# Attention and two feed-forward layers: one output copy on ScalarE, its halves moved by GpSimd, a longer argmax chain, four score products in a slot

## The chip, the cores and the metric

One core of a Trainium2 chip. The metric is the device time of one execution in microseconds. The engines are named TensorE (PE, with PEld for its weight loads), VectorE (DVE), ScalarE (ACT), GpSimd (POOL) and SyncE (SP, which here only issues DMAs).

## The reference

Three stages follow each other: a clustered attention, and two feed-forward layers that differ in their function. Batch 2, 8 heads, 768 positions, head size 64, 16 centroids per head; 1536 tokens, model width 512, hidden width 2048.

```python
q_assign = np.argmax(np.einsum('bhsd,hcd->bhsc', q_n, c_n), axis=-1)   # normalised q, centroids
k_assign = np.argmax(np.einsum('bhsd,hcd->bhsc', k_n, c_n), axis=-1)
mask = q_assign[:, :, :, None] == k_assign[:, :, None, :]
scores = scale * np.matmul(q, k.transpose(0, 1, 3, 2))
scores = np.where(mask, scores, -1000000000.0)
scores = scores - np.max(scores, axis=-1, keepdims=True)
attn = np.exp(scores)
attn = attn / (np.sum(attn, axis=-1, keepdims=True) + 1e-09)
out = np.matmul(attn, v)
...
h = x @ w_in;  g = h * np.cos(h);  x = g @ w_out                       # first layer
g = np.where(pos, h, np.where(neg, 0.0, (h + beta) ** 2 / (4.0 * beta))) # second layer
```

## The kernel before

Every product is made in parts: a value is split into a high part of type fp32r and the rest, so that products of the parts add up to more than fp32r alone gives.

**Attention** goes over 8 pairs of heads (batch x 4). A pair has four units, one for each head h and half hf of its 768 queries, in the order (h0,hf0), (h0,hf1), (h1,hf0), (h1,hf1): 32 units. A unit has six slots, one for each block of 128 keys: 192 slots, and the loop at the end of the stage runs over them. A block n of 128 queries (three in a unit, 96 in all) gets four score products of 384 columns in two steps (`scores`, L471 and L474, tile s, two buffers of two PSUM banks), a maximum over 768 scores on VectorE (`row_max`, L480, tile nm), and an exp on ScalarE (`row_exp`, L489, tile p, six buffers). It is worked on 8 slots (LEAD) ahead of the slot that uses it. In a slot, `p_transpose` turns three 128x128 pieces of p on TensorE (L517, tile pt; the pool ps_t has three banks, which pt shares with the tiles of the preparation and with r), ScalarE copies them as high part phi (L520), and VectorE makes the low part plo (L525, `p_lo`, for two slots at a time in every even slot). `p_v` multiplies phi and plo with the values (L535, L536) into tile o, of which there is one bank; PV_AT lists at which slot after a unit's first each of its six key blocks is multiplied.

When the last of the six is in, `o_parts` empties o. The bank holds 128 rows: the 64 of this head and 64 of the other part of the values. ScalarE copies each half on its own (L549, 64x384) into the rows of this head of two tiles xt0 and xt1, so that for both heads of a pair xt0 and xt1 come to hold what has to be added. Two slots later `finish` transposes the reciprocals rb (L559, tile r), adds the two tiles on GpSimd (L561), multiplies by r on VectorE (L562), and GpSimd splits the result into xh and xl (L565, L569), the input of the first layer. `inverse` makes the reciprocals of the row sums (L499, L500) and GpSimd spreads each of three columns over 64 (L504).

Beside that, `prep_pair` prepares the next pair in small steps, one for each `yield` and slot: transposes of q and k (L329, L337), their parts on GpSimd (L301, L302), DMAs on SP's queue that stack them (L315), the load of the next q and k (L208), products with the centroids (L367, L368, tile pd), their sums (L356, tile dots), and the argmax chain: maximum (L413), compare (L415), a product with falling numbers on GpSimd (L416), maximum (L421), equality (L423). Then come the parts of v (L436, L437), the transposes of the one-hot rows (L446, tile po), their copy (L448, tile oht) and eight DMAs of it into the stacks (L292). A preparation starts PREP slots before the pair ahead of it does (PREP1 for the first).

`later(n, f)` puts a function off until the n-th next call of `next_slot`, of which there is one in each slot, after the value products; `later(1, ...)` from `p_v` so runs in the same slot. The program's text gives the order in which steps are preferred; the order in which each engine gets them is planned when the program is built, and each engine then keeps to it. Weights of the layers are converted by `pump` in steps (L144 to L160), the first twelve in the last 36 slots of attention.

**The layers** (L670 to L672, 512 columns each) follow; TensorE starts the first of them while the last outputs of attention are still being finished.

Of the kernel before, what the change touches and what calls it, by code (L numbers as in the profile page):

```python
# [8 lines left out]
F32 = mybir.dt.float32  # L9
# [4 lines left out]
AF = mybir.ActivationFunctionType  # L14
ALU = mybir.AluOpType
# [3 lines left out]
P = 128  # L19
# [13 lines left out]
def attention_moe_moe(  # L33
# [18 lines left out]
    nc = tc.nc  # L52
    B, H, S, D = q.shape
# [4 lines left out]
    HJ = NJ // 2  # L58
    HS = S // 2
# [9 lines left out]
    cpool = ctx.enter_context(tc.tile_pool(name="cpool", bufs=1))  # L69
# [2 lines left out]
    desc = cpool.tile([P, C], F32, name="desc")  # L72
    for c in range(C):
        nc.gpsimd.memset(desc[:, c:c + 1], float(C - c))
    ones = cpool.tile([P, D], F32, name="ones")
    nc.gpsimd.memset(ones, 1.0)
    ohscale = cpool.tile([P, 1], F32, name="ohscale")
    ohbias = cpool.tile([P, 1], F32, name="ohbias")
    for r in range(4):
# [25 lines left out]
    def later(n, f, *args):  # L105
        due.setdefault(now[0] + n, []).append((f, args))
# [85 lines left out]
    with ExitStack() as actx:  # L192
        ap = actx.enter_context(tc.tile_pool(name="apool", bufs=1))
# [82 lines left out]
        def prep_pair(i):  # L276
# [3 lines left out]
            t = nat[i][0]  # L280
            if i in (1, 3, 5):
                t2 = w0pool.tile([P, 2, 2, S], F32R, tag="w_0", name=f"t2_{i}")
# [78 lines left out]
            for s in range(2):  # L361
                pd = ps_t.tile([P, NJ, 2, 2, C], F32, tag="t", name=f"pd{i}_{s}")
                for j in range(NJ):
                    cols = slice(j * P, (j + 1) * P)
                    o = pd[:, j].rearrange("p t h c -> p (t h c)")
# [11 lines left out]
            if i == 0:  # L377
                run_idle(NIDLE[2], ins(mm))
                for s in range(2):
                    dv = dotv[s]  # L380
                    m = mx[:, s * G // 2:(s + 1) * G // 2].rearrange("p (j h) -> p j h", h=2)
                    e = eq[:, s * G // 2:(s + 1) * G // 2].rearrange("p (j h) c -> p j h c", h=2)
                    mb = m.unsqueeze(3).to_broadcast([P, NJ, 2, C])
                    db = desc.unsqueeze(1).unsqueeze(1).to_broadcast([P, NJ, 2, C])
                    nc.vector.tensor_reduce(m, dv, AX.X, ALU.max)
                    nc.vector.tensor_tensor(e, dv, mb, ALU.is_ge)
                    nc.vector.tensor_tensor(e, e, db, ALU.mult)
                    nc.vector.tensor_reduce(m, e, AX.X, ALU.max)
                    nc.vector.tensor_tensor(dv, e, mb, ALU.is_equal)

                    po = ps_t.tile([P, HJ, P], F32, tag="t", name=f"po0_{s}")
                    for jp in range(HJ):
                        mm = nc.tensor.transpose(
                            po[:4 * C, jp],
                            dv[:, 2 * jp:2 * jp + 2].rearrange("p r h c -> p (r h c)"), ident)
                    run_idle(NIDLE[3 + s], ins(mm))
                    for h in range(2):
                        for par in range(2):
                            r0 = par * 2 * C
                            dst = st[h][s][D:D + 2 * C, 1].rearrange(  # L400
                                "c (jp par n) -> c jp par n", par=2, n=P)[:, :, par]
                            src = po[r0:r0 + 2 * C]
                            if s == 0:
                                nc.scalar.activation(dst, src, AF.Copy)
                            else:
                                nc.vector.tensor_scalar(
                                    dst, src, own[r0:r0 + 2 * C, 0, h:h + 1],
                                    own[r0:r0 + 2 * C, 1, h:h + 1], ALU.mult, ALU.add)
            else:
                dv = dots.rearrange("p j s h c -> p (j s h) c")  # L410
                mb = mx.unsqueeze(2).to_broadcast([P, G, C])
                yield
                nc.vector.tensor_reduce(mx, dv, AX.X, ALU.max)  # L413
                yield
                nc.vector.tensor_tensor(eq, dv, mb, ALU.is_ge)  # L415
                nc.gpsimd.tensor_tensor(  # L416
                    eq, eq, desc.unsqueeze(1).to_broadcast([P, G, C]), ALU.mult)
                yield
                yield
                yield  # L420
                nc.vector.tensor_reduce(mx, eq, AX.X, ALU.max)  # L421
                yield
                nc.vector.tensor_tensor(dv, eq, mb, ALU.is_equal)  # L423
                yield
            if i == 0:
                with tc.issue_after(ins(last[0])):
# [34 lines left out]
        def scores(n, step):  # L461

            i, h, hf = units[n // HJ]
            j = hf * HJ + n % HJ
            qt, kt = prepped[i][1][h]
            if step == 0:
                ptile[n] = ps_s.tile([P, 2, 512], F32, tag="s", name=f"s{n}")
            s = ptile[n]
            cols = slice(j * P, (j + 1) * P)
            kc = slice(step * HS, (step + 1) * HS)  # L470
            nc.tensor.matmul(s[:, step, :HS], qt[:, 0, cols], kt[:, 0, kc],  # L471
                             start=True, stop=False)
            rows = D + C if i else D + 2 * C
            nc.tensor.matmul(s[:, step, :HS], qt[:rows, 1, cols], kt[:rows, 1, kc],  # L474
                             start=False, stop=True)

        def row_max(n):
            nm = ap.tile([P, 1], F32, tag="nm", bufs=8, name=f"nm{n}")
            s = ptile[n]
            nc.vector.tensor_reduce(nm, s[:, :, :HS], AX.XY, ALU.max, negate=True)  # L480
            ptile[n] = (s, nm)

        def row_exp(n):
            s, nm = ptile[n]
            u, jj = divmod(n, HJ)
            if jj == 0:
                dens[u] = ap.tile([P, HJ, 2], F32, tag="den", bufs=4, name=f"den{u}")
            p = ap.tile([P, 2, HS], F32, tag="p", bufs=P_BUFS, name=f"p{n}")
            nc.scalar.activation(p, s[:, :, :HS], AF.Exp, bias=nm,  # L489
                                 accum_out=dens[u][:, jj, 0:1])  # L490
            ptile[n] = p
            if jj == HJ - 1:
                later(2, inverse, u)

        def inverse(u):

            i, h, hf = units[u]
            den = dens.pop(u)
            nc.gpsimd.tensor_scalar(den[:, :, 0], den[:, :, 0], 1e-9, 1.0, ALU.add, ALU.mult)  # L499
            nc.vector.reciprocal(den[:, :, 1], den[:, :, 0])  # L500
            if h == 0:
                rb[(i, hf)] = ap.tile([P, HJ, 2, D], F32, tag="rb", bufs=2, name=f"rb{i}_{hf}")
            for jj in range(HJ):
                nc.gpsimd.tensor_scalar(rb[(i, hf)][:, jj, h], ones, den[:, jj, 1:2], 1.0,  # L504
                                        ALU.mult, ALU.mult)

        dens = {}
        rb = {}
        pts = {}
        xt = {}  # L510
# [29 lines left out]
        def o_parts(u):  # L540
            i, h, hf = units[u]
            o = opsum.pop(u)
            main = slice(h * D, (h + 1) * D)
            other = slice((1 - h) * D, (2 - h) * D)
            if h == 0:
                xt[(i, hf)] = [ap.tile([P, HS], F32, tag=f"xt{n}", bufs=2,
                                       name=f"xt{n}_{i}_{hf}") for n in range(2)]
            for t, rows in zip(xt[(i, hf)], (main, other)):
                nc.scalar.activation(t[main], o[rows], AF.Copy)  # L549
            if h == 1:  # L550
                later(2, finish, i, hf)

        def finish(i, hf):
            b, hp = pairs[i]
# [16 lines left out]

        LEAD, PREP, PREP1 = 8, 12, -3
        PV_AT = (4, 4, 5, 6, 7, 8)
        NSLOT = len(units) * NJ
        PAIR = 4 * NJ
        ct = centroid_load()
# [15 lines left out]
        for slot in range(-max(LEAD, PREP), NSLOT + PV_AT[-1] - NJ + 1):  # L594
            g = slot + LEAD
            if slot in prep_at:
                preps.append(prep_pair(prep_at[slot]))
            if 0 <= slot < NSLOT:
                p_transpose(slot // NJ, slot % NJ)
            if 0 <= g < NSLOT:  # L600
                scores(g // 2, g % 2)
            for u, kt in pv_slots.get(slot, ()):
                p_v(u, kt)
            if slot % 2 == 0:
                for s in (slot - 1, slot):
                    if 0 <= s < NSLOT:
                        p_lo(s // NJ, s % NJ)
                if 2 <= g < NSLOT + 2:
                    row_exp(g // 2 - 1)
            next_slot()  # L610
            if slot == 60:
                issue_chunk(0)
            preps = [p for p in preps if next(p, 0) != 0]
            if NSLOT - 6 * CHUNK <= slot < NSLOT and slot % 3 == 0:
                pump(1)
            if slot % 2 == 1 and 0 <= g < NSLOT:
                row_max(g // 2)
        flush()


# [100 lines left out]
    for l in range(2):  # L721
        for qi in range(NQ):
            for blk in range(NB):
                g = hidden(l, qi, blk)
# [35 lines left out]
```

## Time and profile before

| | before |
|---|---|
| time, median of 3 runs | 823.03 us (818.95 to 823.06) |
| profiled execution: its time, its span | 821.92 us, 819.9 us |
| TensorE busy | 801.3 us (98%), 4042 matmuls |
| VectorE, ScalarE, GpSimd busy | 633.6 (77%), 416.5 (51%), 271.5 us (33%) |
| granted TensorE clock | full in all of the 40 slices |

The page's slices show the stages: attention from about 22 to 284 us, with VectorE and ScalarE at eight to nine tenths and GpSimd at three to seven; then the layers, with ScalarE at two to four tenths and TensorE full. A busy share of TensorE is read with care: records of matmuls overlap and their ends are modelled, so that the spacing of their starts tells more than their length.

### The profile page before, as it was taken

The numbers are of one execution on the slowest core, as the hardware profiler recorded it, in microseconds if no ns is written. First come the engines' busy times: TensorE is split into PE (matmuls) and PEld (weight loads), VectorE is DVE, ScalarE is ACT, GpSimd is POOL, SyncE is SP. The second block draws the span as 40 slices with busy tenths as digits, with TensorE's granted clock in tenths as the row PEclk, the third lists the DMA queues.
The fourth block names the chain that finished last, engine by engine and source line by source line (L and its number), as shares of the span: only waits on it lengthen the run. The fifth ranks groups of instructions, "written<-read, shape, count | busy, mean of one in ns | idle before, by whom it ended". The sixth has DMA issues, their size and how long they took to land.

```text
span 819.9 us, 11334 instructions
## 1 busy us (share of the span) xinstructions
PE 801.3 (98%) x4042; PEld 669.9 (82%) x4042; DVE 633.6 (77%) x957; ACT 416.5 (51%) x794; POOL 271.5 (33%) x442
## 2 busy tenths in 40 slices
PE   8899999999999999999999999999999999999998
PEld 5788988988888887888888888888888888888886
DVE  4889899899898687787878878887876987755552
ACT  3688888897979764444343424323434333222220
POOL 3356665577553341222211221442231122111110
PEclk9999999999999999999999999999999999999999
DMA  7666556446540002222131312122112122000012
GB/s 155 153 131 142 134 129 167 101 105 137 138 88 34 1 13 92 102 68 87 51 104 52 103 56 98 52 81 74 52 54 100 52 78 76 1 1 0 14 49 92
DMA packets 48183, 65.97 MB, mean 80 GB/s; under 512 B 27904, under 2 KB 32640, under 8 KB 48128
## 3 DMA queue, kind: packets, MB, share of 16 engines
q1 hardware_dynamic: 47984, 65.22, 29.2%
q8 instruction: 32, 0.52, 0.3%
q14 instruction: 23, 0.19, 0.1%
q10 hardware_dynamic: 144, 0.03, 0.0%
HBM read 43.02 MB, written 3.15 MB: 56 GB/s over the span
## 4 chain that ended last, share of the span: by engine, by line
PE 62%; DVE 1%; ACT 1%; POOL 1%; issue 0%; POOLq 0%
PE y L672 11%; PE y L671 11%; PE y L670 11%; PE h L672 10%; PE h L671 10%; PE h L670 10%; DVE gl L632 0%; DVE r L640 0%; POOL gh L628 0%; DVE g L645 0%; ACT L641 0%; ACT r L641 0%; DVE w L160 0%; ACT n L639 0%; ACT wx L144 0%
## 5 line engine op out<-in xcount | busy, mean ns | idle before, releaser
L628 POOL TENSOR_SCALAR gh<-g 128x512 fp32r<-128x512 f32 x96 | 71.2, 742 | 292.9 <-DVE g L659 165.7
L671 PE MATMUL h<-xl,w 128*128 128x512 f32 x384 | 151.4, 394 | 0.0
L670 PE MATMUL h<-xh,w 128*128 128x512 f32 x384 | 151.4, 394 | 0.0
L672 PE MATMUL h<-xh,w 128*128 128x512 f32 x384 | 151.3, 394 | 0.0
L525 DVE TENSOR_TENSOR plo<-pt,phi 128x384 fp32r<-128x384 f32 x192 | 99.9, 548 | 17.2 <-ACT phi L520 16.2
L520 ACT ACTIVATE phi<-pt 128x384 fp32r<-128x384 f32 x192 | 91.8, 494 | 21.6 <-PE pt L517 19.8
L655 ACT ACTIVATE p<-h,mone 128x512 f32<-128x512 f32 x48 | 33.1, 689 | 134.5 <-DVE m L654 134.1
L517 PE MATMUL pt<-ident,p 128*128 128x128 f32 x576 | 96.5, 277 | 3.4 <-ACT oht L448 1.6
L480 DVE TENSOR_REDUCE nm<-s 128x1 f32<-128x768 f32 x96 | 90.7, 947 | 6.2 <-PE s L474 5.8
L489 ACT ACTIVATE p<-s,nm 128x768 f32<-128x768 f32 x96 | 86.9, 905 | 10.4 <-DVE nm L480 10.1
L632 DVE TENSOR_TENSOR gl<-g,gh 128x512 fp32r<-128x512 f32 x96 | 71.1, 742 | 20.3 <-POOL gh L628 15.3
L672 PEld LDWEIGHTS h<-xh,w 128*128 128x128 f32 x384 | 71.8, 187 | 17.7
L671 PEld LDWEIGHTS h<-xl,w 128*128 128x128 f32 x384 | 71.8, 187 | 17.6
L670 PEld LDWEIGHTS h<-xh,w 128*128 128x128 f32 x384 | 71.8, 187 | 17.5
L144 ACT ACTIVATE wx<-wraw 128x1024 f32<-128x1024 f32 x32 | 36.4, 1138 | 95.0 <-DMA wraw<-in_moe_w_in_dram 35.4
L471 PE MATMUL s<-st,st 128*128 128x384 f32 x192 | 78.1, 408 | 4.1 <-ACT p L489 3.6
L517 PEld LDWEIGHTS pt<-ident,p 128*128 128x128 f32 x576 | 69.9, 140 | 12.4 <-ACT oht L448 3.3
L672 PE MATMUL y<-gh,w 128*128 128x512 f32 x192 | 74.8, 390 | 1.2 <-DVE w L160 1.2
L671 PE MATMUL y<-gl,w 128*128 128x512 f32 x192 | 74.8, 390 | 0.0
L671 PE MATMUL y<-w,gh 128*128 128x512 f32 x192 | 74.8, 390 | 0.0
L670 PE MATMUL y<-gh,w 128*128 128x512 f32 x192 | 74.8, 389 | 0.0
L670 PE MATMUL y<-w,gh 128*128 128x512 f32 x192 | 74.7, 389 | 0.0
(120 smaller groups left out, 1629.2 us busy)
## 6 DMA issues: line engine op xcount, KB each, us to landing
wraw<-in_moe_w_in_dram SPq DMA_DIRECT2D x16, 1024.0 KB, 5.2
wraw<-in_moe_w_out_dram SPq DMA_DIRECT2D x16, 1024.0 KB, 4.9
st<-t SPq DMA_DIRECT2D x24, 192.0 KB, 4.1
st<-th SPq DMA_DIRECT2D x9, 384.0 KB, 3.8
st<-tl SPq DMA_DIRECT2D x18, 192.0 KB, 4.0
st<-th SPq DMA_DIRECT2D x18, 192.0 KB, 3.2
nat<-in_q_dram SPq DMA_DIRECT2D x8, 384.0 KB, 5.2
nat<-in_k_dram SPq DMA_DIRECT2D x8, 384.0 KB, 5.2
```

The costliest lines, as they stand in the source:

```text
L144: nc.scalar.activation(x, high.bitcast(F32), AF.Abs)
L471: nc.tensor.matmul(s[:, step, :HS], qt[:, 0, cols], kt[:, 0, kc], start=True, stop=False)
L480: nc.vector.tensor_reduce(nm, s[:, :, :HS], AX.XY, ALU.max, negate=True)
L489: nc.scalar.activation(p, s[:, :, :HS], AF.Exp, bias=nm, accum_out=dens[u][:, jj, 0:1])
L517: nc.tensor.transpose(ps[:, jj * P:(jj + 1) * P], p[:, kt * P:(kt + 1) * P], ident)
L520: nc.scalar.activation(hi, ps, AF.Copy)
L525: nc.vector.tensor_tensor(lo, ps, hi.bitcast(F32), ALU.subtract)
L628: nc.gpsimd.tensor_scalar(hi, g, 1.0, 0.0, ALU.mult, ALU.add)
L632: nc.vector.tensor_tensor(lo, g, hi.bitcast(F32), ALU.subtract)
L670: nc.tensor.matmul(o, lh, rh, start=first, stop=False)
L671: nc.tensor.matmul(o, lh, rl, start=False, stop=False)
L672: nc.tensor.matmul(o, ll, rh, start=False, stop=last)
```

## The change

Six edits, all in attention:

- `o_parts` copies the whole bank, 128x384, by one ScalarE instruction into a tile of the head: xt0 for the first, xt1 for the second.
- A new function `o_rows`, a slot after the second head's copy, has GpSimd copy three halves of 64 rows so that two tiles come to hold what is to be added: the first head's other half and the second head's other half change rows into a new tile xt2 and xt1. `finish` comes a slot after that, so at the same slot as before.
- `inverse` fills the 3 x 64 columns of rb by one GpSimd instruction that reads the three reciprocals in a broadcast, instead of three that multiply a tile of ones; the tile of ones goes.
- The argmax chain has three more waiting slots, and PREP is 15 for 12, PREP1 -6 for -3.
- Both steps of a block's scores, four products, come in the even slots; the maximum follows at the end of the same slot and the exp at the end of the odd one.
- PV_AT is (5, 5, 6, 7, 8, 8) for (4, 4, 5, 6, 7, 8).

```diff
-    ones = cpool.tile([P, D], F32, name="ones")
-    nc.gpsimd.memset(ones, 1.0)
...
                 yield
                 yield
                 yield
+                yield
                 nc.vector.tensor_reduce(mx, eq, AX.X, ALU.max)
                 yield
                 nc.vector.tensor_tensor(dv, eq, mb, ALU.is_equal)
+                yield
+                yield
                 yield
...
-            for jj in range(HJ):
-                nc.gpsimd.tensor_scalar(rb[(i, hf)][:, jj, h], ones, den[:, jj, 1:2], 1.0,
-                                        ALU.mult, ALU.mult)
+            nc.gpsimd.tensor_scalar(
+                rb[(i, hf)][:, :, h], den[:, :, 1].unsqueeze(2).to_broadcast([P, HJ, D]),
+                1.0, 0.0, ALU.mult, ALU.add)
...
-            if h == 0:
-                xt[(i, hf)] = [ap.tile([P, HS], F32, tag=f"xt{n}", bufs=2,
-                                       name=f"xt{n}_{i}_{hf}") for n in range(2)]
-            for t, rows in zip(xt[(i, hf)], (main, other)):
-                nc.scalar.activation(t[main], o[rows], AF.Copy)
+
+            t = ap.tile([P, HS], F32, tag=f"xt{h}", bufs=2, name=f"xt{h}_{i}_{hf}")
+            xt.setdefault((i, hf), []).append(t)
+            nc.scalar.activation(t, o, AF.Copy)
             if h == 1:
-                later(2, finish, i, hf)
+                later(1, o_rows, i, hf, main, other)
+
+        def o_rows(i, hf, main, other):
+            t0, t = xt[(i, hf)]
+            t2 = ap.tile([P, HS], F32, tag="xt2", bufs=1, name=f"xt2_{i}_{hf}")
+            xt[(i, hf)] = (t, t2)
+            for dst, rows, src in ((t2, other, t0[main]), (t2, main, t[other]), (t, other, t0[other])):
+                nc.gpsimd.tensor_scalar(dst[rows], src, 1.0, 0.0, ALU.mult, ALU.add)
+            later(1, finish, i, hf)
...
-        LEAD, PREP, PREP1 = 8, 12, -3
-        PV_AT = (4, 4, 5, 6, 7, 8)
+        LEAD, PREP, PREP1 = 8, 15, -6
+        PV_AT = (5, 5, 6, 7, 8, 8)
...
-            if 0 <= g < NSLOT:
-                scores(g // 2, g % 2)
+            if 0 <= g < NSLOT and g % 2 == 0:
+                scores(g // 2, 0)
+                scores(g // 2, 1)
             for u, kt in pv_slots.get(slot, ()):
                 p_v(u, kt)
             if slot % 2 == 0:
                 for s in (slot - 1, slot):
                     if 0 <= s < NSLOT:
                         p_lo(s // NJ, s % NJ)
-                if 2 <= g < NSLOT + 2:
-                    row_exp(g // 2 - 1)
             next_slot()
...
-            if slot % 2 == 1 and 0 <= g < NSLOT:
-                row_max(g // 2)
+            if 0 <= g < NSLOT:
+                (row_exp if g % 2 else row_max)(g // 2)
```

## Rows read from the trace of the kernel before

**Rows 1.** Busy time of each engine, 40 to 280 us: us (x instructions).

```profile
40.00:280.00 240.00, 231.44 (x1536) 208.72 (x1535) 213.66 (x368) 203.72 (x453) 136.73 (x243) 1.00 0.49 113
```

**Rows 2.** Timeline of TensorE, 150 to 153 us: start, us, instruction.

```profile
150.37 0.49 PE L517 MATMUL pt<-ident,p 128*128 128x128 f32 x3
...
151.40 0.49 PE L517 MATMUL pt<-ident,p 128*128 128x128 f32 x3
...
152.58 0.28 PE L367 MATMUL pd<-cn,t 128*128 128x64 f32 x1
152.69 0.28 PE L368 MATMUL pd<-cn,t 128*128 128x64 f32 x1
```

**Rows 3.** TensorE's groups, 40 to 280 us: line, shapes, count, busy, mean ns, idle before.

```profile
L517 PE MATMUL pt<-ident,p 128*128 128x128 f32 x542 | 90.3, 277 | 2.8 <-ACT oht L448 1.6 <-DVE plo L525 1.3
L471 PE MATMUL s<-st,st 128*128 128x384 f32 x176 | 71.9, 409 | 2.6 <-ACT p L489 2.0
L535 PE MATMUL o<-phi,vv 128*128 128x384 f32 x181 | 66.2, 366 | 2.4 <-ACT xt L549 2.3
```

**Rows 4.** Waits, 40 to 280 us: who for whom, us, times, longest.

```profile
PEld s L471 <- ACT p L489: 7.5, 19, 0.6
PEld o L535 <- ACT xt L549: 6.8, 16, 0.7
...
PEld pt L517 <- ACT oht L448: 3.3, 7, 0.5
...
PE o L535 <- ACT xt L549: 2.3, 7, 0.4
...
PE s L471 <- ACT p L489: 2.0, 9, 0.4
PE pt L517 <- ACT oht L448: 1.6, 6, 0.3
```

**Rows 5.** Timeline, 131 to 136 us: a unit's end, its bank, its output.

```profile
131.28 0.34 PE L536 MATMUL o<-plo,vv 128*128 128x384 f32 x1
...
131.65 0.98 ACT L549 ACTIVATE xt<-o 64x384 f32<-64x384 f32 x2 [0.16 <-PE o L536]
...
132.69 0.44 PE L535 MATMUL o<-phi,vv 128*128 128x384 f32 x1 [0.39 <-ACT xt L549]
...
135.46 0.56 DVE L562 TENSOR_TENSOR xt<-xt,r 128x384 f32<-128x384 f32 x1
```

**Rows 6.** GpSimd's groups, 40 to 280 us.

```profile
L504 POOL TENSOR_SCALAR rb<-ones,den 128x64 f32<-128x64 f32 x90 | 28.7, 338 | 5.1 <-DVE den L500 4.6 <-DMA st<-oht 0.6
...
L436 POOL TENSOR_SCALAR vv<-natv 128x384 fp32r<-128x384 f32 x12 | 6.0, 512 | 0.8 <-PE o L536 0.8
```

**Rows 7.** The chain of work that ended last, 284 to 312 us: its add.

```profile
285.85 1.02 POOL xt L561
```

**Rows 8.** Waits, 284 to 312 us.

```profile
PE y L672 <- DVE w L160: 1.2, 1, 1.2
```

**Rows 9.** Two lines of VectorE, whole run: duration in ns, min/median/max.

```profile
L415 DVE TENSOR_TENSOR eq<-dots,mx x7: 546/727/1097, 42.5 to 229.9; 128x384 f32<-128x384 f32 x7
...
L413 DVE TENSOR_REDUCE mx<-dots x7: 514/553/554, 41.2 to 227.7; 128x24 f32<-128x384 f32 x7
```

**Rows 10.** Timeline, 120 to 132 us: VectorE and ScalarE at maxima and exps.

```profile
120.53 1.01 DVE L525 TENSOR_TENSOR plo<-pt,phi 128x384 fp32r<-128x384 f32 x2
120.64 0.90 ACT L489 ACTIVATE p<-s,nm 128x768 f32<-128x768 f32 x1 [1.08 <-DVE nm L480]
...
121.45 0.95 DVE L480 TENSOR_REDUCE nm<-s 128x1 f32<-128x768 f32 x1
...
121.77 0.49 ACT L520 ACTIVATE phi<-pt 128x384 fp32r<-128x384 f32 x1
...
122.44 0.90 ACT L489 ACTIVATE p<-s,nm 128x768 f32<-128x768 f32 x1 [0.17 <-DVE nm L480]
...
123.33 0.48 ACT L520 ACTIVATE phi<-pt 128x384 fp32r<-128x384 f32 x1
```

## Prediction

> **What bounds the kernel now.** I began with the page's busy shares (TensorE 98%) and its chain of work, which is TensorE through both feed-forward layers from about 310 us on; no edit reaches them, so what matters is the attention stage. There I took the busy time of each engine in the stretch 40 to 280 us [rows 1]: TensorE 231.4 of 240 us, VectorE 213.7, ScalarE 203.7, GpSimd 136.7. A busy TensorE is not a full one, so next comes what it would need without a wait. In an undisturbed slot the transposes of one slot start 1.03 us after those of the slot before, with three transposes and four products of 384 columns between; the 64-column products follow each other by 0.11 us [rows 2]. The stretch holds 542 transposes of the probabilities, 2 x 176 score products and 2 x 181 value products [rows 3], that is 542 / 3 = 180.7 slots x 1.03 = 186.1 us; the other 279 small instructions (1536 less these and one of the next stage, [rows 1]) at 0.11 us are 30.7. Sum 216.8: TensorE loses some 23 of 240 us, and a slot takes 1.33 us on average.
>
> The waits tell to whom [rows 4]: score products waiting for the exp that frees their bank (2.0 us on the matmuls, 7.5 on their weight loads, 19 loads), value products waiting for the copies that empty the one output bank (2.3 and 6.8, 16 loads), transposes waiting for the one-hot copy (1.6 and 3.3, 7). The matmul figure is too low, since a record runs 0.34 us where the next start comes after 0.17, and hides that much of each wait; the load figure is too high, since loads run ahead. I count the first plus 0.17 us per load that waited: output bank 2.3 + 16 x 0.17 = 5.0; scores 2.0 + 19 x 0.17 = 5.2; one-hot 1.6 + 7 x 0.17 = 2.8. Together 13.0 of the 23 us; the rest is many small gaps behind ScalarE and VectorE, which are nearly as loaded as TensorE.
>
> **The change, part by part.** *One output copy.* The bank is now read by two copies back to back, 0.98 us, and the value product that reopens it started 132.69, 0.39 us late, its load 0.71 [rows 5]. One 128x384 copy instead of two of 64x384 frees it 0.49 us sooner; in that case the 0.39 is gone. ScalarE is relieved of 32 x 0.49 = 15.7 us, 14.7 of them in the stretch (30 x 0.49). The new list of value slots also opens the next unit at its slot 11 instead of 10: between the last value product and that opening stand the transposes of three slots and four score products, 3 x 0.33 + 4 x 0.175 = 1.69 us (a slot's 1.03 split by 0.11 and 0.175), instead of two slots' and the same four, 1.36. So 0.49 + 0.33 = 0.82 us of room are added, and no load waited over 0.7 [rows 4]. I take 5.0 to 0.5, gain **4.5** (bounds 2.5, if only half the cases are reached, and 6.8).
>
> *Copies on GpSimd.* Added are 16 x 3 copies of 64x384. The nearest row is the copy of 128x384 at 512 ns; two rows bound it, 338 ns for 64 columns [rows 6] and 1.02 us for two inputs [rows 7]. I take 0.51 since the columns are equal: 24.6 us. The 96 reciprocal fills of 338 ns become 32 of 192 columns, between 338 and 512, say 0.40: 32.4 us down to 12.8. GpSimd gains 5 us over the whole stage on 57% load, and the dropped memset of ones is one short instruction at the start. What hides the three copies: now the product with the reciprocals starts 4.18 us after the last value product did, at 135.46 against 131.28 [rows 5]. The new way, from the product's end at 131.62: copy 0.03 + 0.49, three GpSimd copies 1.53 with some 0.08 ahead of each of the two that depend, and ahead of the first and of the add, the add 1.02, and 0.03 more: 3.4 us, so 135.05, under 135.46. The cover is 0.4 us. If it goes, the reciprocals' bank (one of three that the transposes share) and VectorE's queue wait: 16 x 0.4 = 6 us at most. I take 0.5.
>
> *The end of attention* has no such cover. The chain of work there runs from the add at 285.85 [rows 7] without a break to the weight part of the first output products, and TensorE idles 1.2 us for it [rows 8]. The new chain is 1.53 + 4 x 0.08 longer less 0.49 and the hop that both have, 0.08: **+1.3** (0 if VectorE makes it up, 1.5 at most).
>
> *Argmax chain.* Seven waiting slots become ten, the preparation starts three earlier (15 for 12; for the first pair 6 for 3). So transposes, the stack's DMAs on SP's queue, the next load of q and k, the dot sums, the first maximum, the compare and GpSimd's product move three slots ahead, the second maximum and the equality two; the one-hot transposes, their copy and its eight DMAs, and v's split stay. On SP's queue the next stack comes three slots (4 us) nearer to the eight one-hot copies ahead of it; should it wait for them, it still has over twenty slots until its first score product, so nothing is taken for it. TensorE's transposes no longer meet an equality that is just being made: 2.8 to 0.8, gain **2.0** (bounds 0 and 3.3). For the first pair, two copies and two differences come in between the first exps; 0 taken, 1 us either way.
>
> *Four score products a slot.* The same products; TensorE does one group per two slots. A group after transposes costs no more than one after products, since the slot of 1.03 us has both. Maximum and exp of a block come a slot and half a slot earlier against the reuse of the bank, 0.7 us or more where the waits averaged 0.4 (7.5 / 19). But VectorE and ScalarE still have 214 and 189 us to do in 230, so half of the lost time comes back as another wait: gain **2.6** of 5.2 (0 to 5.2).
>
> Sum: -4.5 - 2.0 - 2.6 + 0.5 + 1.3 = **-7.3 us**. On the profiled execution, 821.9 us with a span of 819.9, that is 814.6. The median of the three runs is 823.0, 1.1 above it, the fastest 818.95 below it; I put the forecast at **815.0**.
>
> **A rule against the change.** VectorE's compare with two inputs in SBUF took 546 to 1097 ns, a maximum with one 514 to 554 [rows 9]: something holds the first, by 0.17 us in the median (727 less 553 ns). The Trainium skill, page "SBUF — State Buffer", section "Who interferes with whom", says that such an instruction and a GpSimd one that reads SBUF exclude each other for a whole instruction. The trace agrees in kind. The added copies read SBUF, but the 64 fewer fills count against them; were each of the 14 two-input steps held by one copy more, VectorE would pay 14 x 0.51 = 7 us, and the gain would be gone. That is a case of the first rival.
>
> **Rivals.**
> *The gain is taken back.* VectorE (89% busy) becomes the bound, whether by its own load, by the cover of 0.4 us failing (6 us) or by GpSimd's copies in its way (7 us). For it: its load [rows 1], and that slots become uneven, eight products in one and none in the next. Against: ScalarE, whose work most of the waits name, loses 14.7 us. Time: 821.9 - 7.3 + 6.5 = 821.
>
> *A loop between ScalarE and VectorE, slower.* In the new text the exp stands behind the copies of its two slots and ahead of the next. Then one round is: copy 0.49, low part 0.46 (two take 0.92, from 120.53 to 121.45), maximum to exp 0.99 (121.45 to 122.44), exp to next copy 0.89 (122.44 to 123.33) [rows 10]: 2.83 us for two slots, against 2.66 now (240 / 90.3). Before, the exp stood one maximum later and the loop spread over two rounds. It decides from the point at which the exp is ahead of the next copy in every round: 96 x 0.17 = 16 us, plus the other work on VectorE that falls ahead of the maximum, half of 213.7 - 90.3 x (1.01 + 0.95) = 36.7, 18 us. Time 838 to 856. For it: the two low parts and then the maximum stand in these rows as in the text. Against: the order on the engines is not strictly the text's; between the exps at 120.64 and 122.44 stands one copy, where the text has two [rows 10], so a step that is ready goes ahead of one that is not, and that breaks the loop whenever TensorE is one slot ahead.
>
> *More is gained.* All 13.0 us of waits go and the small gaps shrink with ScalarE's load (3 us): 821.9 - 16 + 1.8 = 808.
>
> **How the numbers follow.** Forecast 0.55, taken back 0.25, loop 0.12, more 0.08. What a measurement here can tell from no change is 0.5%, 4 us: 819 to 827. Faster: nearly all of the forecast, more, and a third of taken back: 0.66; same: 0.22; slower: the loop, 0.12. The range leaves out the loop and a little at each end: low 807, from the larger gain; high 823, from taken back with both of its prices.
>
> **What would show it.** Right: the waits of value products for the output copy nearly gone, score waits halved, one-hot waits under 1 us, ScalarE near 189 us in a stretch of the same work, the last maximum some 8 us earlier, TensorE's idle at the first output products 2.5 us. Wrong: VectorE waiting for GpSimd's add, transposes waiting for low parts or for the reciprocals' product, or exps that stand 2.8 us apart with copies waiting behind them.

## The result

The changed kernel takes **831.44 us** (median, 824.81 to 835.07) against 821.94 us (818.95 to 823.18) in the same comparison: a ratio of 1.0125 [1.0102, 1.0148], so **slower by 1.25%** where 815 us, faster by 0.9%, was forecast. The profiled execution took 831.01 us with a span of 829.2. All of the loss is in attention: the last of the 96 maxima starts at 283.67 us (before 275.37), while from the first output product of the first layer to the last of the second it is 509.4 us against 509.3. (One execution of e11_spread, the one that was traced, was disturbed and took 1577.61 us, where the other ten have a median of 816.4; e13_spread_again is the same kernel again, with a trace.)

The waits of 40 to 280 us answer to [rows 4]; columns as there.

```profile
DVE xt L570 <- POOL xt L569: 21.7, 14, 2.8
PEld pt L518 <- DVE xt L570: 15.3, 7, 2.5
PE pt L518 <- DVE xt L570: 13.5, 7, 2.2
...
PEld s L472 <- ACT p L490: 3.2, 11, 0.5
PE pt L518 <- DVE plo L526: 2.1, 6, 0.5
...
PE s L472 <- ACT p L490: 0.2, 1, 0.2
```

The three waits that the change aims at have fallen: score products for the exp from 2.0 to 0.2 us on the matmuls (7.5 to 3.2 on the loads), value products for the output copy from 2.3 to nothing, transposes for the one-hot copy from 1.6 to nothing. In place of these waits TensorE's transposes wait 13.5 us, in seven pieces, for the product of the outputs with the reciprocals (L570), and VectorE, which makes it, waits 21.7 us for GpSimd's add. Before, that wait of VectorE was 0.6 us in one place.

One such place, from the timeline of the changed kernel (start, us, engine, instruction, idle before and its releaser). It is the end of a pair's last unit.

```profile
64.14 0.34 PE L537 MATMUL o<-plo,vv 128*128 128x384 f32 x1
...
64.56 0.99 POOL L437 TENSOR_SCALAR vv<-natv 128x384 fp32r<-128x384 f32 x2 [0.81 <-PE o L537]
...
64.69 0.48 ACT L549 ACTIVATE xt<-o 128x384 f32<-128x384 f32 x1
...
65.52 2.29 POOL L438 TENSOR_TENSOR vv<-natv,vv 128x384 fp32r<-128x384 f32 x2
...
65.99 0.49 PE L567 MATMUL r<-ident,rb 128*128 128x128 f32 x3
...
67.89 1.10 POOL L558 TENSOR_SCALAR xt<-xt 64x384 f32<-64x384 f32 x2
...
69.07 0.99 POOL L569 TENSOR_TENSOR xt<-xt,xt 128x384 f32<-128x384 f32 x1
...
70.10 0.55 DVE L570 TENSOR_TENSOR xt<-xt,r 128x384 f32<-128x384 f32 x1 [2.34 <-POOL xt L569]
...
70.71 0.55 PE L518 MATMUL pt<-ident,p 128*128 128x128 f32 x3 [1.86 <-DVE xt L570]
```

The copy on ScalarE is done at 65.17. One of the three copies on GpSimd needs only the first head's bank and stood earlier in GpSimd's order (62.81 us). The two others could start at 65.17, but GpSimd has just begun to split the values for the pair after next (L437, L438: four instructions, until 67.8). The buffer for them is one of two, and what frees it is the same value product that completes this output bank: the split and the copies become ready together, at the end of every pair from the first to the sixth. So the two start at 67.89, 2.7 us late, the add at 69.07, and VectorE stands for 2.34 us ahead of the product. r holds one of the three banks of the transposes from 65.99 on. No maximum and no low part goes past on VectorE, which keeps its order: the maximum that follows at 70.57 had its scores at 66.15. So TensorE stops for 1.86 us. In the trace there are six such stops, one each pair from 70.71 to 246.26 us, of 1.86 to 2.20 us. At the end of the seventh pair, where no split follows, the product starts 2.92 us after the last value product's end, for 5.62 here.

What follows a stop is a second loss. TensorE's starts behind the one above, then the clock by stretches of 20 us (busy time of PE, PEld, DVE, ACT, POOL with their counts; then the granted clock, the DMA share and GB/s):

```profile
73.16 0.52 PE L472 MATMUL s<-st,st 128*128 128x384 f32 x1
73.47 0.52 PE L475 MATMUL s<-st,st 80*128 80x384 f32 x1
73.80 0.52 PE L472 MATMUL s<-st,st 128*128 128x384 f32 x1
```

```profile
40.00:60.00 20.00, 19.67 (x137) 17.68 (x136) 15.42 (x28) 14.32 (x34) 9.95 (x16) 1.00 0.69 143
60.00:80.00 20.00, 17.80 (x108) 16.08 (x107) 15.16 (x28) 14.85 (x33) 13.42 (x24) 0.91 0.59 121
80.00:100.00 20.00, 19.88 (x140) 18.48 (x138) 16.87 (x31) 15.79 (x36) 10.83 (x18) 1.00 0.43 115
```

Products of 384 columns follow each other by 0.31 to 0.33 us, where they had done so by 0.175: the clock is at 1.2 instead of 2.4 GHz for a while. Five stretches show 0.91 (the others are 100 to 120, 160 to 180, 200 to 220 and 240 to 260), and each holds one of the six stops; the sixth stop, at 140.99 us and 2.13 long, has no such stretch behind it. No stretch of the profiled execution of before shows less than 1.00. The executions of the changed kernel differ by it: 824.8 and 828.9 us at a mean clock of 0.997, 833.2 and 835.1 at 0.983 and 0.982. That is (834.1 - 826.9) / 0.0145 = about 5 us for each 0.01. By that estimate some 5 of the 9 us of the profiled execution, at 0.99, are the clock, and the rest is what the stops cost beyond what the fallen waits gave. It is a correlation over eight executions and no more; a mean clock does not tell where the clock fell. Before has it too: of its executions beside the experiments about one in five stood at 0.991 to 0.993 and took 823.0 us in the mean, the others 820.0; in e12's trace, at 0.992, the fall lies in the first 40 us.

### The profile page after: what moved, and what is told of

The parts are those of the page before. It is cut to its first block, busy times and chain, and to the rows that moved or that the text cites. A ratio compares the mean times of both kernels' runs of the same rounds, so it can differ in the third digit from the quotient of the medians.

```text
span 829.2 us, 11220 instructions
## 1 busy us (share of the span) xinstructions
PE 800.5 (97%) x4041; PEld 674.6 (81%) x4042; DVE 630.8 (76%) x957; ACT 402.3 (49%) x762; POOL 280.1 (34%) x425
## 4 chain that ended last, share of the span: by engine, by line
PE 78%; POOL 8%; DVE 7%; ACT 4%; issue 3%; DMA 0%; POOLq 0%; DVEq 0%; ACTq 0%
PE y L679 10%; PE y L678 10%; PE y L677 10%; PE h L677 10%; PE h L678 10%; PE h L679 10%; PE pt L518 5%; PE s L472 2%; PE s L475 2%; POOL xt L558 2%; PE o L537 2%; POOL xt L569 2%; PE o L536 2%; POOL vv L438 1%; DVE nm L481 1%
## 5 line engine op out<-in xcount | busy, mean ns | idle before, releaser
L518 PE MATMUL pt<-ident,p 128*128 128x128 f32 x576 | 99.3, 286 | 16.5 <-DVE xt L570 13.5
L639 DVE TENSOR_TENSOR gl<-g,gh 128x512 fp32r<-128x512 f32 x96 | 71.6, 746 | 19.6 <-POOL gh L635 14.5
L472 PE MATMUL s<-st,st 128*128 128x384 f32 x192 | 74.8, 391 | 2.5 <-ACT p L490 2.1
L677 PE MATMUL y<-gh,w 128*128 128x512 f32 x192 | 74.9, 390 | 1.1 <-POOL w L155 1.1
L716 DVE TENSOR_TENSOR acc<-y,acc 128x512 f32<-128x512 f32 x72 | 49.3, 686 | 34.0 <-PE y L679 34.0
```

The lines of the kernel that those rows point to most:

```text
L518: nc.tensor.transpose(ps[:, jj * P:(jj + 1) * P], p[:, kt * P:(kt + 1) * P], ident)
L639: nc.vector.tensor_tensor(lo, g, hi.bitcast(F32), ALU.subtract)
L677: nc.tensor.matmul(o, lh, rh, start=first, stop=False)
L716: nc.vector.tensor_tensor(a, po, a, ALU.add)
```

## The experiments

The theory, from the trace: **GpSimd's line**. Two copies stand in GpSimd's order behind the split of the values, and the add and a sum for the reciprocals behind the copies; VectorE in its order stops at the first of its steps that needs one of them, then TensorE, then the clock falls. (Its line is the order in which GpSimd takes its instructions.) The rival: **uneven slots**, eight products in one slot and none in the next, which leave VectorE and TensorE without cover.

**The parts on either side.** e1 keeps everything but the copies:

```diff
...
-            nc.scalar.activation(t, o, AF.Copy)
...
+            for t, rows in zip(xt[(i, hf)], (main, other)):
+                nc.scalar.activation(t[main], o[rows], AF.Copy)
             if h == 1:
-                later(1, o_rows, i, hf, main, other)
...
+                later(2, finish, i, hf)
```

> The changed kernel with the outputs copied as before: two ScalarE copies of 64x384 a unit, no copies on GpSimd, the sum two slots later; the score slots, the value slots, the longer argmax chain and the broadcast fill stay. Theory Q (the three copies stand in GpSimd's queue with the split of v, the add comes late, VectorE stops at the product with the reciprocals and TensorE's transposes stop for its bank): VectorE's 21.7 us of waiting for the add fall under 4, TensorE's 13.5 us for that product under 1, no stretch at 1.2 GHz, time 810 to 820. Rival S (the uneven slots lose the time): the waits move to other names and the time stays at 826 or more.

e2 is the kernel before with only the new copies: the one on ScalarE and the three on GpSimd.

> The kernel before with one edit alone: one ScalarE copy of the whole output bank and three GpSimd copies a slot later. Theory Q: VectorE waits 15 to 22 us for the add, TensorE stops for the product's bank, time 827 to 835. Rival S: the slots are those of before, so 818 to 823, a little under before by the ScalarE copies that go.

Measured: e1 817.77 us (816.79 to 818.87), ratio 0.9967 [0.9951, 0.9982]; e2 835.32 us (834.15 to 838.29), ratio 1.0193 [1.016, 1.0226]. The copies alone make more than the whole loss, and the rest without them is a small gain: as the cause of the loss the rival of the uneven slots falls. e2's waits in 40 to 280 us:

```profile
DVE xt L569 <- POOL xt L568: 14.5, 8, 2.5
...
PE po L446 <- DVE den L500: 9.2, 5, 2.2
```

VectorE stops at the same product for 14.5 us, a little under the 15 to 22 expected; TensorE stops at the one-hot transposes and not, as expected, at the bank of r. In e2's trace, at a mean clock of 0.992, only two of the twelve stretches of 20 us from 40 to 280 show 0.91, and yet it loses over 12 us to before: there most of the loss is not the clock.

But the gain without them is 0.33%, 2.7 us, where the forecast had 4.6 for slots and chain. Two of e1's expectations were missed: VectorE still waits 5.1 us for the add (under 4 expected) and TensorE 3.2 for the product (under 1). Its waits in 40 to 280 us show where the rest went:

```profile
DVE xt L563 <- POOL xt L562: 5.1, 4, 1.5
PEld s L472 <- ACT p L490: 4.9, 15, 0.7
PEld pt L518 <- DVE plo L526: 4.8, 10, 1.0
PEld pt L518 <- DVE xt L563: 4.4, 5, 1.2
...
PE pt L518 <- DVE xt L563: 3.2, 4, 0.9
PEld o L536 <- ACT xt L550: 2.1, 5, 0.7
PE pt L518 <- DVE plo L526: 2.0, 5, 0.7
```

The loads' waits for ScalarE's copies and exps are 7.0 us (before 14.3, [rows 4]); in their place 9.2 us of loads wait for two steps of VectorE.

**Where VectorE stops.** If only the product stood too early, to have it a slot or two later would do. In e3 `finish` comes three slots after `o_rows` instead of one:

```diff
-            later(1, finish, i, hf)
+            later(3, finish, i, hf)
```

> The changed kernel with the sum, the transposes of the reciprocals and the product put off by two more slots (three instead of one after the GpSimd copies); nothing is left out. Theory Q: two slots are 2.6 us, as long as the longest wait of 2.8, so VectorE waits under 5 us for the add, TensorE's clock stays at 2.4 GHz, time 815 to 823. Rival S: 826 or more.

Measured: 830.5 us (828.55 to 830.97), ratio 1.0124 [1.0097, 1.0151]: no better than the change, and a miss of the expectation, in the clock too (0.987 to 0.989). Its waits, 40 to 280 us:

```profile
DVE den L501 <- POOL den L500: 25.2, 20, 2.7
PEld pt L518 <- DVE plo L526: 17.8, 14, 2.3
PE pt L518 <- DVE plo L526: 14.3, 12, 2.1
```

The product waits no more, but the same time is lost at the reciprocals of the row sums (L501), whose sum with 1e-9 GpSimd makes (L500) behind the same line, and the transposes now wait for the low parts behind it on VectorE. What counts is the line, not which step of VectorE meets it. So in e4 the line ahead of the add is made shorter: the split of the values is put behind the outputs' add in GpSimd's order (`added[0]` is that add):

```diff
...
+            with tc.issue_after(ins(added[0])) if added[0] is not None else ExitStack():
                 for h in range(2):
                     hi = vv[:, :, 3 * D * h:3 * D * h + D]
                     ...
...
-            nc.gpsimd.tensor_tensor(t1, t1, t2, ALU.add)
+            added[0] = nc.gpsimd.tensor_tensor(t1, t1, t2, ALU.add)
```

> The changed kernel with the split of v on GpSimd put behind the add of the outputs in GpSimd's order; nothing is left out. Theory Q, if it is the split that stands in the way: the waits of the second half's product (2.3 to 2.8 us each) come down to those of the first half (0.6 to 1.0), VectorE waits 10 to 13 us for the add instead of 21.7, TensorE under 4 us for the bank, the clock stays up, time 819 to 825. If the three copies by themselves are too long, the waits stay at 2 us and the time at 828 or more. Rival S: 826 or more.

Measured: 822.03 us (819.46 to 823.44), ratio 1.0015 [0.9995, 1.0034]. An order alone, with no work removed, takes back 1.0125 - 1.0015 = 1.1%, 9 us, with an uncertainty of 2.5 (here and below from the two 95% intervals). Its clock was 0.999 or more in nine executions of ten and 0.992 in one; the stops that are left are six of 1.05 to 1.38 us and one of 0.85. VectorE's wait for the add is 7.5 us, under the 10 to 13 expected, and TensorE's 0.9. The six are the reciprocals':

```profile
DVE den L503 <- POOL den L502: 16.8, 14, 1.8
PEld pt L520 <- DVE plo L528: 15.2, 19, 1.7
PE pt L520 <- DVE plo L528: 9.9, 11, 1.4
...
DVE xt L572 <- POOL xt L571: 7.5, 12, 1.0
```

One of them in the timeline: the sum with 1e-9 (L502) now stands behind copies, add and split, and starts at 70.16 us, where it started at 70.15 in the changed kernel.

```profile
68.11 1.97 POOL L440 TENSOR_TENSOR vv<-natv,vv 128x384 fp32r<-128x384 f32 x2
...
70.16 0.20 POOL L502 TENSOR_SCALAR den<-den 128x3 f32<-128x3 f32 x1
...
70.39 0.18 DVE L503 RECIPROCAL den<-den 128x3 f32<-128x3 f32 x1 [1.76 <-POOL den L502]
```

**The line taken apart.** e11 goes two steps on from e4: VectorE makes the sum for the reciprocals itself, and the copy that needs only the first head's bank is put a unit earlier, behind that head's copy on ScalarE, by the text (in e4 the planned order had drawn it forward anyway, to 62.31 us at the place shown above):

```diff
-            nc.gpsimd.tensor_scalar(den[:, :, 0], den[:, :, 0], 1e-9, 1.0, ALU.add, ALU.mult)
+            nc.vector.tensor_scalar(den[:, :, 0], den[:, :, 0], 1e-9, 1.0, ALU.add, ALU.mult)
...
-            if h == 1:
-                later(1, o_rows, i, hf, main, other)
+            later(1, o_row if h == 0 else o_rows, i, hf, main, other)
+        def o_row(i, hf, main, other):
+            t2 = ap.tile([P, HS], F32, tag="xt2", bufs=2, name=f"xt2_{i}_{hf}")
+            xt[(i, hf)].append(t2)
+            nc.gpsimd.tensor_scalar(t2[main], xt[(i, hf)][0][other], 1.0, 0.0, ALU.mult, ALU.add)
...
```

> The changed kernel with GpSimd's pile taken apart: the split of v behind the outputs' add, the sum of 1e-9 for the reciprocals on VectorE, and one of the three copies a unit earlier, behind the first output copy. If what is left of the loss at 822.0 us (the split moved alone) is VectorE waiting for GpSimd's sum for the reciprocals, this gives 815 to 819, with VectorE's waits for GpSimd under 5 us of the stretch in all. If GpSimd's copies cost by being there (in VectorE's way at the memory), 820 to 824.

> The kernel of e11_spread (817.75 us, ratio 0.9951) beside e14, for its trace and a comparison on one chip. If what VectorE waited for was all that the copies cost, its waits for GpSimd in the stretch are under 5 us in all and the time is 815 to 819. The forecast's one copy, 4.5 us, would put it 4 to 5 us under e14; if the wait of the value products had only passed on, within 2 us of e14.

e14 has the same order and the same sum on VectorE, but two copies on ScalarE and none on GpSimd, so that e13 against e14 is the price or gain of the one output copy by itself.

> The same as e13 but with two ScalarE copies a unit and no copies on GpSimd: slots, longer chain, the one fill, the split of v behind the add, the sum of 1e-9 on VectorE. 816 to 820; with 820 or more if the one copy is worth its 4.5 us, 816 to 818 if it is worth under 2.

Measured: e11 817.75 us, ratio 0.9951 [0.993, 0.9972]; e13, the same kernel again, 816.87 us (813.79 to 818.27), ratio **0.9946** [0.9925, 0.9967]; e14 818.97 us, ratio 0.9981 [0.9962, 1.0]. This is the version that beats both kernels, by 0.5% against before and 1.8% against the change. e13's waits, 40 to 280 us:

```profile
PEld pt L520 <- DVE plo L528: 11.7, 20, 1.6
DVE xt L575 <- POOL xt L574: 8.0, 13, 1.2
...
PE pt L520 <- DVE plo L528: 5.8, 9, 1.2
```

No value product waits for its copy, and VectorE's waits for GpSimd are 8.0 us, down from 27.7 with the reciprocals' 6.0 (the expectation said under 5). The two steps, the sum and the earlier copy, were not tried apart. The one copy is worth 0.9981 - 0.9946 = 0.35%, 2.9 us, with an uncertainty of about 2.3 (2.1 us by the medians): between the two forecasts for e13, neither the full 4.5 nor clearly nothing.

**Is it the split's place alone?** Two kernels without copies on GpSimd: e7 is e1 with e4's order, e8 is the kernel before with it.

> The changed kernel with two ScalarE copies again in place of the copies on GpSimd, and with the split of v put behind the outputs' add in GpSimd's order. If GpSimd's queue is what holds VectorE, the 7.8 us that VectorE still waits for the add without the copies (817.8 us) fall below 2 us, and the time is 813 to 816. If that wait had no one behind it, 817 to 819.

> The kernel before with the split of v put behind the outputs' add alone. VectorE waits for the add only 0.6 us of the stretch there, so the theory expects no change: 819 to 822. A gain of over 3 us would mean that the split stood in the way before too, and that the changed kernel lost something else; a loss of over 3 us that a later split holds the value products.

Measured: e7 818.39 us, ratio 0.9973 [0.9954, 0.9993], no better than e1 (0.9967); e8 820.1 us, ratio 0.9994 [0.9973, 1.0015]. The split's place is worth nothing where no copies stand behind it. e7 was expected at 813 to 816 and did not get there: VectorE's wait for the add, 5.1 us in e1, is gone, but its wait for the sum for the reciprocals is 9.8 us instead of 4.1. It had passed to the next step in line, which stands behind the split in either order.

**Slots and chain, one by one.** e5 is the kernel before with the new slots (four score products, the places of maximum and exp, PV_AT), e6 with the longer argmax chain, e9 with both, e12 with the one reciprocal fill. The edits of e5, e6, e9 and e12 are those hunks of the change's diff. e10 is e6 with the preparation a slot later and one waiting slot fewer behind the equality:

```diff
                 nc.vector.tensor_tensor(dv, eq, mb, ALU.is_equal)
                 yield
                 yield
-                yield
...
-        LEAD, PREP, PREP1 = 8, 15, -6
+        LEAD, PREP, PREP1 = 8, 14, -5
```

> The kernel before with the new slots alone: four score products a slot, the places of the maximum and the exp, and the value products a slot later. The forecast's sum gave this part 2.6 us; if the parts add up, 817 us. If one engine's wait only passes to the next (the theory by now: what ScalarE gives up, VectorE takes), 819 to 823, with the waits of score products for the exp well under the 7.5 us of before on the loads and the transposes' waits for the low parts in their place. If the uneven slots cost something by themselves, over 824.

> The kernel before with the three more waiting slots in the argmax chain alone (preparation 15 slots ahead, 6 less for the first pair). The forecast's sum gave it 2.0 us, so 818 if the parts add up; 819 to 822 if the transposes' wait for the one-hot copy (1.6 us on the matmuls, 3.3 on the loads) goes and another takes its place. Over 823 only if the moved steps meet something new at their earlier place.

> The kernel before with the new slots and the longer argmax chain together, without the new output copies and with the old reciprocal fills. Alone the slots gave 824.4 us and the chain 828.1, and both with the new fill 817.8. If slots and chain only work together (each moves ScalarE's steps by one slot, so that alone they meet each other's), 816 to 820. If it is the shorter fill that turned 3 and 7 us of loss into 3 of gain, 824 to 832.

> The chain-alone kernel (828.1 us) with the preparation 14 instead of 15 slots ahead (5 instead of 6 less for the first pair) and one waiting slot fewer, so that its copies on ScalarE stand at slots of the same parity as before, with the exp where it was. If the odd shift is what cost the 7 us, 819 to 823; if the early place itself did, 825 to 829.

> The kernel before with the one reciprocal fill of 192 columns in place of three of 64. It takes some 10 us of work off GpSimd, which bounds nothing: 820 to 822. 816 to 818 if the reciprocals' late fill held the transposes.

| kernel | us, median | ratio to before |
|---|---|---|
| e5, slots | 824.35 | 1.0042 [1.002, 1.0063] |
| e6, chain | 828.12 | 1.0094 [1.0058, 1.013] |
| e10, chain a slot later | 825.34 | 1.0052 [1.002, 1.0085] |
| e9, slots and chain | 819.77 | 0.9993 [0.9976, 1.0009] |
| e12, fill | 822.58 | 1.0017 [0.9998, 1.0036] |

Either part alone makes the kernel slower, and both together are no change: the parts do not add up, and neither has the gain that the forecast gave it. So the new slots do cost something by themselves (e5, over 824 by a little), though not the loss of the change. One wait in e5 that before does not have is of the one-hot transposes for the equality:

```profile
PE po L446 <- DVE dots L423: 3.1, 3, 1.6
```

The longer chain makes the equality earlier against these transposes, and e9 shows no such wait. That this is why the two only go together is argued from the waits; no run tests it. e5's score products still wait for the exp 2.5 us on the matmuls and 6.7 on the loads, little under before. The waits of e6, 40 to 280 us, against [rows 4]:

```profile
PEld s L474 <- ACT p L492: 8.8, 24, 0.9
PEld o L538 <- ACT xt L552: 8.6, 22, 0.8
PE pt L520 <- DVE plo L528: 4.4, 8, 0.7
...
PE s L474 <- ACT p L492: 2.5, 9, 0.6
PE o L538 <- ACT xt L552: 2.4, 10, 0.4
...
PEld pt L520 <- ACT oht L451: 1.4, 6, 0.2
```

By the prediction's way of counting (matmuls, and 0.17 us for each load) the one-hot copy costs 6 x 0.17 = 1.0 us instead of 2.8, the gain that was forecast; but the exp costs 2.5 + 24 x 0.17 = 6.6 instead of 5.2, the output copies 2.4 + 22 x 0.17 = 6.1 instead of 5.0, and the matmuls' wait for low parts, 1.3 before, is 4.4. What the preparation does on ScalarE and VectorE has only come to meet other steps. Whether it is that it now falls on odd slots, as e10 was to tell, stays open: e10's median lies at the lower end of the second expectation (825 to 829), and its interval overlaps that of e6. That it takes the shorter fill to undo the loss of slots and chain is refuted by e9, which does so without it. What the fill adds to them, e1 against e9, is 0.26%, 2.1 us with an uncertainty of 1.9; alone it gains nothing (e12).

## Why the prediction was wrong, point by point

**What bounds the kernel.** TensorE with losses to ScalarE's copies and exps and to the one-hot copy: the three waits did fall when their causes were removed, in the changed kernel nearly to nothing. The reading of the rows held; that a fallen wait is time gained did not.

**The step that failed: the cover of GpSimd's copies.** The prediction compared two chains, 4.18 us then and 3.4 us new, called the difference a cover of 0.4 us, and priced its failing at 16 x 0.4 = 6 us at most. The new chain was sized well: at the outputs in the middle of a pair, where GpSimd has no split to make, the product starts 2.9 to 3.2 us after the last value product's end (4.4 at the first of the eight). But the 4.18 us were no free chain. At the end of a pair GpSimd was then splitting the values as well, as its timeline in the kernel before shows at a pair's end:

```profile
66.82 0.99 POOL L436 TENSOR_SCALAR vv<-natv 128x384 fp32r<-128x384 f32 x2
67.78 1.00 POOL L437 TENSOR_TENSOR vv<-natv,vv 128x384 fp32r<-128x384 f32 x1
68.75 1.01 POOL L561 TENSOR_TENSOR xt<-xt,xt 128x384 f32<-128x384 f32 x1
69.73 1.01 POOL L437 TENSOR_TENSOR vv<-natv,vv 128x384 fp32r<-128x384 f32 x1
```

The add was ready at 66.71, when the last of the copies had ended, and started at 68.75, amid the split. The output of [rows 5] is such an end too. The split is 3 us of GpSimd's work there, and two copies of 0.55 us, one behind the other, come on top of it. The prediction worked out what the copies wait for, but not what else stands in GpSimd's order at that moment. It also named VectorE's queue and the bank as those who would wait, rightly, and then took the price of the delay for one step of 0.4 us, where what stops is TensorE, some 2 us at a time, in six places. From the runs the term of +0.5 us is about 14.7, with an uncertainty of 2.6: 9.0 between the change and e4 (the split in the way) and (1.0015 - 0.9946) x 821 = 5.7 between e4 and e13 (the sum for the reciprocals behind the line, which was VectorE's longest wait for GpSimd in e4, and the earlier copy; the first is likely the most of it, since in e4 the copy ran early anyway, but they were not measured apart).

**The clock** was not in the forecast, since the trace of before shows full speed in every stretch. By the estimate above it is some 5 us of the profiled execution, a part of the 14.7 and not beside it.

**One output copy, -4.5.** Measured apart from GpSimd's line: -2.9 with an uncertainty of 2.3 (e13 against e14). That is near the lower of its bounds, 2.5 and 6.8. ScalarE is busy 188.0 us of the stretch in e13, against the 189 named. The room for the value products was as worked out: none waits in the changed kernel.

**Four score products -2.6, argmax chain -2.0.** Together 0.6 us of gain, with an uncertainty of 1.4 (e9), and alone +3.4 and +7.7 us. The prediction took half of the score waits back for a new wait and none of the chain's; the runs give nearly all of both back. To cost each part by the wait it removes treats the waits as independent, while VectorE and ScalarE, at 214 and 204 us of 240 [rows 1], pass much of the time on, as the waits of e1, e5 and e6 show. This was the first rival's mechanism, and it is what happens without the copies (e1 817.8 us, e9 819.8, for the 821 that it was given); its piece "the cover of 0.4 us failing" is the cause of the loss, at a price more than twice its 6 us.

**GpSimd's work.** Copies: 538 ns in the mean (510 in the median) for the 0.51 taken, and the fill 361 ns for the 0.40, from GpSimd's groups of the changed kernel, 40 to 280 us:

```profile
L558 POOL TENSOR_SCALAR xt<-xt 64x384 f32<-64x384 f32 x42 | 22.6, 538 | 48.2 <-ACT xt L549 42.9 <-DMA st<-oht 3.2
...
L504 POOL TENSOR_SCALAR rb<-den 128x192 f32<-128x192 f32 x28 | 10.1, 361 | 7.5 <-DVE den L501 7.0
```

These prices were right, and they were not what mattered.

**The end of attention, +1.3.** From the end of the last value product to the start of the product with the reciprocals it is 297.15 - 293.65 = 3.50 us for 286.89 - 284.75 = 2.14 before: 1.36 longer, as forecast. But the first output product of the first layer comes 22.1 us after that value product against 21.9, so only 0.25 us of it reach TensorE, and the wait of 1.2 us there [rows 8] is 1.1, not 2.5.

**VectorE held by GpSimd's copies at the memory** (the rule of the Trainium skill, page "SBUF — State Buffer", section "Who interferes with whom", priced at 7 us). The steps that it speaks of, with two inputs in SBUF, are the compare and the equality. The compare over the whole run of the changed kernel (duration in ns, min/median/max), then the equality in 40 to 280 us (busy us, mean ns) of the changed kernel and of the kernel before:

```profile
L413 DVE TENSOR_TENSOR eq<-dots,mx x7: 548/558/685, 36.2 to 233.2; 128x384 f32<-128x384 f32 x7
```

```profile
L422 DVE TENSOR_TENSOR dots<-eq,mx 128x384 f32<-128x384 f32 x7 | 4.7, 665 | 0.0
```

```profile
L423 DVE TENSOR_TENSOR dots<-eq,mx 128x384 f32<-128x384 f32 x7 | 5.2, 744 | 0.0
```

The compare takes 558 ns in the median for 727 [rows 9], the equality 665 in the mean for 744. The price of 7 us does not appear: the steps became shorter, with 48 copies more. Both moved to other slots as well, so this does not show that they are never held; e13, with all 48 copies, is faster than e14 with none.

**The loop between ScalarE and VectorE** (838 to 856 us) did not appear: ScalarE's waits for the maximum are 8.3 us in 40 to 280 us of the changed kernel (7.9 before), and e1, e9 and e13, with the exp at the same place in the text, take 817 to 820 us.

## What to carry to other kernels

When work is moved to an engine that is idle half of the time, look up what stands in that engine's order at the very moment at which the moved work becomes ready, above all what the same event releases; the mean load says nothing about it. Then list who waits for that engine and what stands behind them on engines that take their instructions in order: here a delay of 2.7 us on an engine with 57% load stopped VectorE, then TensorE, and the clock stood at half for a while behind it. And a wait that is removed between engines at 85 to 90% load is not a gain until a run shows it: three of them went, priced at 9.1 us together, and with GpSimd's line taken apart the whole kernel gained 4.4 (e13).

## What the runs showed of the hardware

TensorE's clock fell behind stops that were not long. In the changed kernel five of the six stops of 1.86 to 2.20 us lie in stretches of 20 us with a granted clock of 0.91; behind the first, products of 384 columns were 0.31 to 0.33 us apart instead of 0.175, from 72.19 to about 75.6 us. In e4, with six stops of 1.05 to 1.38 us and the same work around them, no stretch of the execution profiled was under 1.00. The length alone does not decide it: the sixth stop of the changed kernel, of 2.13 us, was followed by no fall, nor were one of 1.87 in e3 and two of 1.75 and 1.92 in e2. In these runs, then, a stop of about 2 us mostly cost more than itself.

Half of the partitions cost as much as all of them: on GpSimd 510 ns in the median for a copy of 64x384 and 512 in the mean for one of 128x384 [rows 6], on ScalarE 0.48 us for the copy of 128x384 and 0.98 for two of 64x384 [rows 5].
